# The columns of x and of the gate, taken out of a decode kernel's first load and fetched by 16 small DMAs on ScalarE's queue

## The chip, the cores and the metric

The kernel runs on one core of one Trainium2 chip. The metric is the device time of one execution in microseconds (us); of several runs the median is taken. A profile of one execution stands beside it: its instructions on TensorE (PE, with its weight loads PEld), VectorE (DVE), ScalarE (ACT), GpSimd (POOL) and SyncE (SP), and its DMAs.

## What is computed

One decode step of two attention blocks over the same token, mixed by a gate. Block A has 16 heads with a cache of their own each, block B 16 query heads over 8 cached heads; both have 8192 cached positions of 256 elements, and everything is float32.

```python
g = sigmoid((x * gate_w).sum(-1, keepdims=True))     # x: 1 x 448
# for A (16 cached heads) and B (8 cached heads, each for two query heads):
q = (x @ wq).reshape(heads, 256)
scores = einsum(q, k_cache) * 256 ** -0.5
o = einsum(softmax(scores), v_cache)
y = o.reshape(heads * 256) @ wo
out = g * y_A + (1 - g) * y_B
```

The caches and the weights are 432 MB; x and gate_w are 448 elements each.

## The kernel before

All inputs are laid out in one array in device memory, `stream`, in the order in which the kernel uses them. `plan()` (L47) makes that order: for each of 8 sets of heads a piece of `wq`, then 12 tiles of K (three units of four tiles each; 16 rows of 256 elements on 128 partitions a tile), the V tiles three places behind their K tiles, and the set's piece of `wo`. It cuts this list into loads of `FULL` = 15,872 columns of float32 on 128 partitions. `LOADS` has one entry for each buffer fill; the last fills consist of several smaller loads into regions of one buffer.

The buffers are the three slots of the pool `ring` (`SLOTS = 3`). The loop over `LOADS` at the end of the kernel takes a slot, issues the load's DMA on SP's queue (L468), and then calls `piece` for each piece in it, which writes out the instructions that consume it. The order is as written (`manual_schedule`): the framework adds semaphore waits but moves nothing. A load into a slot waits until the slot's previous contents have been read.

The small operands x and gate_w are called `xg`: each is held as 4 columns on 128 partitions (448 = 3 x 128 + 64, and the last 64 twice), so `XG` = 8 columns, 32 bytes a partition, 4 KB in all. Before, `plan` puts `("xg", 0)` first in the list, and its 8 columns are the first of the first load, which is therefore 15,880 columns wide; every slot has `FULL + XG` columns for that reason. When `piece` meets kind `"xg"`, it calls `inputs` on the first four columns and keeps the other four in `GW[0]`.

`inputs` (L191) copies x into the zeroed tile `xz` with three DVE copies (L192 to L194). `project` (L220) multiplies `xz` with `wq` on PE to give the queries of a set; ScalarE copies them out (L224) and `spread` prepares them. `prepare` computes the gate from `xz` and `GW[0]` (L200 to L205). The scores come from PE (`scores`, L255) or, for one unit of each set, from DVE (`scores_by_row`, L277 and L281), the sums over V from PE (`attend`, L307). Before all that, DVE and POOL make constants (L119 to L182), which needs no load. The output leaves with one DMA of four partitions (L483).

Of the kernel before, what the change touches and what calls it, by code (L numbers as in the profile page):

```python
# [7 lines left out]
F32 = mybir.dt.float32  # L8
# [6 lines left out]
P = 128  # L15
D = 448
DH = 256
SK = 8192
NCOL = SK // P
KF = D // P  # L20
# [5 lines left out]
ROWS = 16  # L26
NT = NCOL // ROWS
FULL = 15872
# [6 lines left out]
WQ = (4 * KF + 2) * DH  # L35
# [5 lines left out]


XG = 2 * (KF + 1)
ATOM = {"xg": XG, "k": 2 * DH, "v": 2 * DH, "wq": 2 * DH, "wo": D}


def plan():  # L47

    size = {"xg": XG, "k": ROWS * DH, "v": ROWS * DH, "wq": WQ, "wo": 8 * D}
    per = len(UNITS) * NT  # L50
    n = len(TILES)
    items = []
    for i in range(n + LEAD):
        if i == 0:
            items += [("xg", 0), ("wq", 0)]
        if i < n:
            items.append(("k", i))
        if i >= LEAD:
            items.append(("v", i - LEAD))
        if i % per == 7 and i // per + 1 < NS:  # L60
            items.append(("wq", i // per + 1))
        if i % per == LEAD + 1 and i >= per:
            items.append(("wo", i // per - 1))
    loads, room = [[]], FULL
    last = [("v", n - 3), ("v", n - 2)]
    for kind, i in items[:items.index(last[0])]:
        at, left = 0, size[kind]
        while left:
            step = min(left, room) // ATOM[kind] * ATOM[kind]
            if step:  # L70
                loads[-1].append((kind, i, at, step))
            at, left, room = at + step, left - step, room - step * (kind != "xg")
            if left:
                loads.append([])
                room = FULL

    loads = [[x] for x in loads]
    x = loads[-2][0]
    loads[-2] = [x[:2], x[2:]]
    loads[-1] += [[(kind, i, 0, size[kind])] for kind, i in last]  # L80
    at, end = 0, []
    for c in LAST_CUT:
        end.append([("v", n - 1, at, c * DH)])
        at += c * DH

    for h, e, n in ((3, 0, 2), (0, 0, 2), (1, 0, 3), (2, 1, 1)):
        end.append([("wo", NS - 1, (2 * h + e) * D, n * D)])
    return loads + [end]


LOADS = plan()


@with_exitstack
def kernel(
# [5 lines left out]
    nc = tc.nc  # L101
    scale = DH ** -0.5

    const = ctx.enter_context(tc.tile_pool(name="const", bufs=1))
    ring = ctx.enter_context(tc.tile_pool(name="ring", bufs=SLOTS))
# [85 lines left out]
    def inputs(xs):  # L191
        nc.vector.tensor_copy(xz[:, :KF, 0], xs[:, :KF])  # L192
        nc.vector.tensor_copy(xz[:KR, KF, 0:1], xs[:KR, KF:])  # L193
        nc.vector.tensor_copy(xz[KR:, KF + 1, 0:1], xs[KR:, KF:])  # L194

    def prepare(gw):
        clear(YY[0], D)
        gp = ps_s.tile([1, 1], F32, name="sm")
        for c in range(KF + 1):
            nc.tensor.matmul(gp, xz[:, c, 0:1], gw[:, c:c + 1], start=(c == 0), stop=(c == KF))  # L200
        ge = const.tile([1, 1], F32, name="ge")
        nc.scalar.activation(ge, gp, AF.Exp, scale=-1.0)
        nc.vector.tensor_scalar(ge, ge, 1.0, None, op0=OP.add)
        nc.vector.reciprocal(gate[:, 0:1], ge)
        nc.vector.tensor_scalar(gate[:, 1:2], gate[:, 0:1], -1.0, 1.0, op0=OP.mult, op1=OP.add)  # L205
# [5 lines left out]
    def project(s, c0, w):  # L211

        if c0 == 0:
            QR[s] = ps_s.tile([2 * BLK, 2 * DH], F32, name="sm")
        q = QR[s]
        for j in range(w.shape[1]):
            a, c = divmod(c0 + j, KF)
            for a in (a,) if a < 2 else (0, 1):
                c = c if c0 + j < 2 * KF else KF
                nc.tensor.matmul(q[BLK * a:BLK * (a + 1), :], xz[:, c if c < KF else KF + a, :], w[:, j, :],  # L220
                                 start=(c == 0), stop=(c == KF), skip_group_check=True)
        if c0 + w.shape[1] == 2 * KF + 1:
            QR[s] = small.tile([P, NB * BLK], F32, name="px")[:2 * BLK, :2 * DH]
            nc.scalar.activation(QR[s], q, AF.Copy)  # L224

    def spread(s):

        qt = ps_s.tile([P, 2, 2, 2], F32, name="sm")
        qr = QR.pop(s)
        for h in range(2):  # L230
            for e in range(2):
                at = h * DH + e * P
                nc.tensor.matmul(qt[:, h, e, :], qr[:, at:at + P], rows4[:2 * BLK, :2], start=True, stop=True)
        for r, a, h, M in ((2, 0, 0, 2), (0, 1, 0, 1), (1, 1, 1, 1)):
            if (s, r) in BY_ROW:
                qa = ps_s.tile([P, DH], F32, name="sm")
                nc.tensor.matmul(qa, spread32, qr[:, h * DH:(h + 1) * DH], start=True, stop=True)  # L237
                QA[s, r] = small.tile([P, DH], F32, name="qa", bufs=1)
                nc.scalar.activation(QA[s, r], qa, AF.Copy, scale=-scale)
                continue  # L240
            nc.vector.tensor_scalar(QB[s % 2, r][:, :, BLK:BLK + M], qt[:, h:h + M, :, a].rearrange("p h e -> p e h"),
                                    -scale, None, op0=OP.mult)
# [56 lines left out]
    def attend(u, t, j0, n, vt):  # L299

        w = 2 * NG * R[heads(u)]
        if t == 0 and j0 == 0:
            O[u] = ps_o.tile([P, 2 * DH], F32, name="o")
        pr = PR[u, t]
        for j in range(j0, j0 + n, 2):
            g = j // 2 % (P // w)
            nc.tensor.matmul(O[u][w * g:w * (g + 1), :], pr[:, j // 2, :w], vt[:, j - j0:j - j0 + 2, :],  # L307
                             start=(t == 0 and j < 2 * P // w), stop=(t == NT - 1 and j >= NB - 2 * P // w),
                             skip_group_check=True)
# [91 lines left out]
    LAST, GW = {}, {}  # L401
# [3 lines left out]
    def wait(n, f, *args):  # L405
        todo.append([n, f, args])

    def tick():
        for t in todo:
            t[0] -= 1  # L410
        for t in [t for t in todo if t[0] <= 0]:
            todo.remove(t)
            t[1](*t[2])

    def piece(kind, i, at, view):
        n = view.shape[-1] // ATOM[kind]
        j0 = at // ATOM[kind]
        if kind == "xg":
            inputs(view[:, :KF + 1])
            GW[0] = view[:, KF + 1:]  # L420
        elif kind == "wq":
            project(i, j0, view.rearrange("p (c n) -> p c n", c=n))
            if j0 + n < 2 * KF + 1:
                pass
            elif i == 0:
                spread(0)
                prepare(GW[0])
            else:
                wait(1, spread, i)
        elif kind == "k":  # L430
            u, t = TILES[i]
            if u in BY_ROW:
                scores_by_row(u, t, 2 * j0, view.rearrange("p (j d) -> p j d", d=DH))
            else:
                scores(u, t, j0, view.rearrange("p (c n) -> p c n", c=n))
            if j0 + n < 2 * NG:
                return
            tick()
            if t == NT - 1:
                gather(u)  # L440
                wait(1, combine, u)
                wait(2, column, u)
        elif kind == "v":
            u, t = TILES[i]
            n = view.shape[-1] // DH
            attend(u, t, at // DH, n, view.rearrange("p (j d) -> p j d", d=DH))
            if at // DH + n == ROWS:
                if t == NT - 1:
                    take(u)
                    if u != TILES[-1][0]:  # L450
                        wait(1, project_o, u)
                if i >= len(TILES) - LEAD:
                    tick()
        elif kind == "wo" and i < NS - 1:
            emit_set(i, j0, view.rearrange("p (c n) -> p c n", c=n))
            if i == NS - 2 and j0 + n == 8:
                fold()
        else:
            for j in range(n):
                LAST[divmod(j0 + j, 2)] = view[:, j * D:(j + 1) * D]  # L460

    off = 0
    for fill in LOADS:
        buf = ring.tile([P, FULL + XG], F32, name="slot")
        c = 0
        for load in fill:
            n = sum(x[3] for x in load)
            nc.sync.dma_start(buf[:, c:c + n], stream[off:off + P * n].rearrange("(p n) -> p n", p=P))  # L468
            off += P * n
            for x in load:  # L470
                piece(*x[:3], buf[:, c:c + x[3]])
                c += x[3]
# [78 lines left out]
```

## Time and profile before

| what | value |
|---|---|
| median of 3 runs | 1010.5 us (1010.24 to 1010.51) |
| span of the profiled execution | 1008.4 us |
| what the median has beyond that span | 2.1 us |
| DMA | 432.49 MB, mean 429 GB/s |
| PE busy | 584.2 us (58%) |
| DVE busy | 458.2 us (45%) |
| ACT busy | 92.8 us (9%) |
| DMA issues by SP | 63 loads at L468, 1 output at L483 |

The span runs from the first to the last instruction of the profiled execution; the time of a run is counted a little wider, and no separate time of the profiled execution is given, so the median stands for it. In the rows, an engine's name with a q (SPq) is its instruction queue, which waits, branches and issues DMAs. A row of the timeline has start, duration, engine, line, operation, output<-input and count; what stands in brackets is how long the engine was idle before it and what ended that. A row of the windows has, for a stretch, the busy time of PE, PEld, DVE, ACT and POOL, the granted clock of PE, the DMA engines' busy share and GB/s. A row of the waits has the total, how often, and the longest.

### The profile page before, as it was taken

What the parts mean: (1) busy time and instruction counts of PE and PEld (TensorE: products, weight loads), DVE (VectorE), ACT (ScalarE), POOL (GpSimd) and SP (SyncE); (2) the same over time, 40 slices, a digit from 0 to 9 for tenths busy, and PEclk for the clock granted to TensorE, in tenths of its full rate; (3) what the DMA queues carried; (4) which work ended last, traced back from release to release, by engine and by line L of the source; (5) the groups of instructions that cost most, each with busy time, mean ns of one, the idle gap of its engine ahead of it and who ended that gap; (6) DMA issues with size and microseconds to landing.
All of it is one profiled execution on the core that took longest, in us unless ns stands there. A gap on an engine that the chain in (4) does not pass through costs nothing.

```text
span 1008.4 us, 7568 instructions
## 1 busy us (share of the span) xinstructions
PE 584.2 (58%) x3154; PEld 171.4 (17%) x3154; DVE 458.2 (45%) x644; ACT 92.8 (9%) x307; POOL 1.9 (0%) x10
## 2 busy tenths in 40 slices
PE   0855845664655555746646576655665637536567
PEld 0211211121111111212111121111211112111112
DVE  1386213961248521576214841248521585206851
ACT  0100100010100110001100000100110100101010
POOL 0000000000000000000000000000000000000000
PEclk9877787777787787877777767776787867877878
DMA  9999999999999999999999999999999999999997
GB/s 403 442 438 418 434 436 439 418 441 431 441 436 426 424 441 438 429 426 442 431 428 441 431 429 434 436 434 431 432 431 441 439 423 424 439 443 431 418 426 310
DMA packets 9113, 432.49 MB, mean 429 GB/s; under 512 B 1016, under 2 KB 1144, under 8 KB 1784
## 3 DMA queue, kind: packets, MB, share of 16 engines
q1 hardware_dynamic: 9080, 432.02, 99.2%
q8 instruction: 24, 0.39, 0.2%
q14 instruction: 9, 0.07, 0.0%
HBM read 432.02 MB, written 0.00 MB: 428 GB/s over the span
## 4 chain that ended last, share of the span: by engine, by line
DMA 72%; DVE 15%; PE 11%; ACT 1%; issue 1%; another core or an unknown queue 0%; SPq 0%; ACTq 0%; DVEq 0%
DMA slot<-in_stream_dram 72%; DVE sr L281 6%; DVE slot L277 6%; PE o L307 5%; PE sc L255 4%; PE sm L220 1%; ACT px L264 0%; DVE mn L261 0%; DVE pr L294 0%; ACT pxr L290 0%; DVE pr L267 0%; ACT ew L346 0%; DVE wr L353 0%; PE sm L371 0%; DVE mt L287 0%
## 5 line engine op out<-in xcount | busy, mean ns | idle before, releaser
L307 PE MATMUL o<-slot,pr 128*32 128x512 f32 (+1 forms) x1536 | 352.4, 764 | 220.2 <-DMA slot<-in_stream_dram 220.2
L255 PE MATMUL sc<-slot,qb 128*32 128x512 f32 x1024 | 199.0, 725 | 102.5 <-DMA slot<-in_stream_dram 102.3
L261 DVE TENSOR_REDUCE mn<-sc 128x1 f32<-128x512 f32 x64 | 44.1, 690 | 334.3 <-PE sc L255 311.5
L277 DVE TENSOR_TENSOR slot<-slot,qa 128x4096 f32<-128x4096 f32 (+7 forms) x40 | 142.6, 3565 | 43.6 <-DMA slot<-in_stream_dram 43.6
L307 PEld LDWEIGHTS o<-slot,pr 128*32 128x32 f32 (+1 forms) x1536 | 80.6, 143 | 403.5 <-DMA slot<-in_stream_dram 249.0
L281 DVE TENSOR_REDUCE sr<-slot 128x16 f32<-128x4096 f32 (+7 forms) x40 | 142.7, 3567 | 1.4
L255 PEld LDWEIGHTS sc<-slot,qb 128*32 128x32 f32 x1024 | 47.1, 132 | 221.2 <-issue 125.5
L264 ACT ACTIVATE px<-sc,st 128x512 f32<-128x512 f32 x64 | 44.0, 687 | 408.1 <-DVE st L262 366.5
L267 DVE STREAM_TRANSPOSE pr<-px 128x512 f32<-128x512 f32 x64 | 45.6, 713 | 59.5 <-ACT px L264 59.5
L220 PE MATMUL sm<-slot,xz 128*32 128x512 f32 x128 | 47.2, 717 | 36.8 <-DVE xz L193 22.9
L290 ACT ACTIVATE pxr<-sr,st 128x16 f32<-128x16 f32 x32 | 9.8, 308 | 372.9 <-DVE st L288 372.9
L371 PE MATMUL sm<-sel,ob 128*128 128x1 f32 (+1 forms) x96 | 18.2, 294 | 36.6 <-DVE ob L317 36.6
L317 DVE SCALAR_TENSOR_TENSOR ob<-o,half,ob 128x256 f32<-128x256 f32 x24 | 11.3, 473 | 43.6 <-ACT ob L316 43.6
L371 PEld LDWEIGHTS sm<-sel,ob 128*128 128x128 f32 x96 | 16.2, 237 | 60.5 <-DVE ob L317 54.9
L220 PEld LDWEIGHTS sm<-slot,xz 128*32 128x32 f32 x128 | 11.3, 129 | 67.0 <-issue 28.4
L294 DVE TENSOR_TENSOR pr<-pxr,cols 128x256 f32<-128x256 f32 x32 | 13.6, 426 | 15.9 <-ACT pxr L290 15.9
L237 PE MATMUL sm<-px,spread 64*128 64x256 f32 x16 | 7.1, 533 | 14.4 <-DVE es L347 14.4
L360 PE MATMUL sm<-ones,wr 1*128 1x1 f32 x48 | 9.6, 268 | 9.2 <-DVE wr L353 9.2
L316 ACT ACTIVATE ob<-o,half 128x256 f32<-128x256 f32 x24 | 11.3, 469 | 39.7 <-PE o L307 39.6
L380 PE MATMUL Y<-slot,ocs 128*1 128x448 f32 x112 | 14.1, 621 | 0.0
L360 PEld LDWEIGHTS sm<-ones,wr 1*128 1x128 f32 x48 | 7.8, 203 | 32.6 <-issue 32.6
L264 ACT ACTIVATION_READ_ACCUMULATOR px<-sc,st 128x1 f32 x64 | 12.3, 193 | 0.0
(73 smaller groups left out, 137.5 us busy)
## 6 DMA issues: line engine op xcount, KB each, us to landing
slot<-in_stream_dram SPq DMA_DIRECT2D x50, 7936.0 KB, 42.5
slot<-in_stream_dram SPq DMA_DIRECT2D x1, 7940.0 KB, 21.8
slot<-in_stream_dram SPq DMA_DIRECT2D x1, 4864.0 KB, 41.2
slot<-in_stream_dram SPq DMA_DIRECT2D x2, 2048.0 KB, 25.3
slot<-in_stream_dram SPq DMA_DIRECT2D x1, 3072.0 KB, 30.1
slot<-in_stream_dram SPq DMA_DIRECT2D x1, 1280.0 KB, 20.8
slot<-in_stream_dram SPq DMA_DIRECT2D x1, 1024.0 KB, 23.5
slot<-in_stream_dram SPq DMA_DIRECT2D x2, 512.0 KB, 24.8
```

The costliest lines, as they stand in the source:

```text
L220: nc.tensor.matmul(q[BLK * a:BLK * (a + 1), :], xz[:, c if c < KF else KF + a, :], w[:, j, :], start=(c == 0), stop=(c == KF), skip_group_ ...
L255: nc.tensor.matmul(sc[32 * g:32 * (g + 1), :], qb[:, e, at:at + 32], kt[:, j, :], start=(e == 0), stop=(e == 1), skip_group_check=True)
L261: nc.vector.tensor_reduce(mn, sc, axis=AX.X, op=OP.min)
L264: nc.scalar.activation(px, sc, AF.Exp, bias=st[:, 0, t:t + 1], scale=-1.0, accum_out=st[:, 1, t:t + 1])
L267: nc.vector.transpose(pr.rearrange("p (q r k) -> p q k r", r=BLK, k=2), px.rearrange("p (q k c) -> p q k c", c=BLK, k=2))
L277: nc.vector.tensor_tensor(kt, kt, QA[u][:, None, :].to_broadcast([P, n, DH]), op=OP.mult)
L281: nc.vector.tensor_reduce(sc[:, j0:j0 + n], kt, axis=AX.X, op=OP.add)
L294: nc.vector.tensor_tensor(pr, px[:, :, None, :].to_broadcast([P, ROWS // 2, NG * NT, 2]), cols[:, t].rearrange("p g r -> p (g r)")[:, None ...
L307: nc.tensor.matmul(O[u][w * g:w * (g + 1), :], pr[:, j // 2, :w], vt[:, j - j0:j - j0 + 2, :], start=(t == 0 and j < 2 * P // w), stop=(t ...
L360: nc.tensor.matmul(cl, WR.pop(u).rearrange("p c x m k -> p (c x m k)"), ones[:1, :], start=True, stop=True)
L371: nc.tensor.matmul(oc[:, e, :M], OB[u][:, e::2], SEL[u][:, :M], start=True, stop=True)
L380: nc.tensor.matmul(YY[0][32 * h:32 * h + 1, :], OC[s, r][:, e, m:m + 1], wt[:, j, :], start=False, stop=(s == NS - 2 and e == 1), skip_gro ...
```

## The change

The kind `"xg"` leaves the plan. The 8 columns get a tile of their own, `xg` in the pool `const`. They stand at the head of `stream`, 128 rows of 32 bytes, and are fetched by 16 DMAs on ScalarE's queue, with 1, 2, 3, ... 15 and then 8 partitions (120 + 8 = 128). These stand in program order ahead of the loop over `LOADS`. `inputs` is called, and `GW[0]` set, right after the first load has been issued, on the new tile. The first load is 15,872 columns wide, as most others are, and the slots are `FULL` columns wide.

```diff
 XG = 2 * (KF + 1)
-ATOM = {"xg": XG, "k": 2 * DH, "v": 2 * DH, "wq": 2 * DH, "wo": D}
+SMALL = list(range(1, 16)) + [8]
+ATOM = {"k": 2 * DH, "v": 2 * DH, "wq": 2 * DH, "wo": D}
...
         if i == 0:
-            items += [("xg", 0), ("wq", 0)]
+            items.append(("wq", 0))
...
-            at, left, room = at + step, left - step, room - step * (kind != "xg")
+            at, left, room = at + step, left - step, room - step
...
-        if kind == "xg":
-            inputs(view[:, :KF + 1])
-            GW[0] = view[:, KF + 1:]
-        elif kind == "wq":
+        if kind == "wq":
...
-    off = 0
+    xg = const.tile([P, XG], F32, name="xg")
+    row = 0
+    for n in SMALL:
+        nc.scalar.dma_start(xg[row:row + n, :], stream[row * XG:(row + n) * XG].rearrange("(p n) -> p n", n=XG))
+        row += n
+
+    off = P * XG
     for fill in LOADS:
-        buf = ring.tile([P, FULL + XG], F32, name="slot")
+        buf = ring.tile([P, FULL], F32, name="slot")
         c = 0
         for load in fill:
             n = sum(x[3] for x in load)
             nc.sync.dma_start(buf[:, c:c + n], stream[off:off + P * n].rearrange("(p n) -> p n", p=P))
             off += P * n
+            if off == P * (XG + FULL):
+                inputs(xg[:, :KF + 1])
+                GW[0] = xg[:, KF + 1:]
             for x in load:
```

More of the change, by code (lines that the diff above doesn't have):

```diff
@@ L43 @@
 XG = 2 * (KF + 1)
-ATOM = {"xg": XG, "k": 2 * DH, "v": 2 * DH, "wq": 2 * DH, "wo": D}
+SMALL = list(range(1, 16)) + [8]
+ATOM = {"k": 2 * DH, "v": 2 * DH, "wq": 2 * DH, "wo": D}
 def plan():
-    size = {"xg": XG, "k": ROWS * DH, "v": ROWS * DH, "wq": WQ, "wo": 8 * D}
+    size = {"k": ROWS * DH, "v": ROWS * DH, "wq": WQ, "wo": 8 * D}
     per = len(UNITS) * NT
@@ L530 @@
     }
-    parts["xg"] = [_np.concatenate([col(get("A_x")), col(get("gate_w"))], axis=1)]
+    xg = _np.concatenate([col(get("A_x")), col(get("gate_w"))], axis=1)
     laid = {
-        "stream": _np.concatenate([
+        "stream": _np.concatenate([xg.ravel()] + [
             _np.concatenate([parts[kind][i][:, at:at + n] for kind, i, at, n in load], axis=1).ravel()
```

## The prediction

> **What bounds the kernel now.** I read the page first: the span, the slices of the DMA engines, the queues and the chain that ended last.
>
> ```profile
> span 1008.4 us, 7568 instructions
> DMA  9999999999999999999999999999999999999997
> q1 hardware_dynamic: 9080, 432.02, 99.2%
> DMA 72%; DVE 15%; PE 11%; ACT 1%; issue 1%; another core or an unknown queue 0%; SPq 0%; ACTq 0%; DVEq 0%
> ...
> slot<-in_stream_dram SPq DMA_DIRECT2D x50, 7936.0 KB, 42.5
> slot<-in_stream_dram SPq DMA_DIRECT2D x1, 7940.0 KB, 21.8
> slot<-in_stream_dram SPq DMA_DIRECT2D x1, 1280.0 KB, 20.8
> ```
>
> The queue's packets fill 99.2% of 16 engines' time. The chain names PE and DVE too, but only because a load is issued when they release a slot; such a load then waits some 42.5 us although a load alone lands in 21.8, so it stands behind another load. The windows confirm that this cover never runs out between start and tail:
>
> ```profile
> 0.00:30.00 30.00, 6.44 (x16) 1.35 (x16) 5.00 (x32) 1.87 (x2) 1.90 (x10) 1.00 0.96 406
> ...
> 60.00:100.00 40.00, 24.22 (x90) 7.15 (x90) 30.05 (x21) 2.21 (x9) 0.00 (x0) 0.71 1.00 432
> 100.00:500.00 400.00, 232.69 (x1270) 68.63 (x1266) 175.73 (x245) 37.45 (x124) 0.00 (x0) 0.76 1.00 433
> 500.00:960.00 460.00, 269.61 (x1407) 78.50 (x1405) 214.42 (x283) 41.30 (x139) 0.00 (x0) 0.75 1.00 432
> 960.00:1008.40 48.40, 31.53 (x263) 9.83 (x262) 15.27 (x33) 5.51 (x19) 0.00 (x0) 0.80 0.86 365
> ```
>
> The last two figures of each row are the DMA share and GB/s: 1.00 at 432 to 433 from 60 to 960 us. The time is therefore the first load's start, plus 432 MB at a fixed rate, plus a short tail. Whatever delays the first load's issue is paid in full, since no later gap could take it up; whatever touches PE, DVE or ACT costs nothing while slots come free early enough.
>
> **How an issue can be held.** Next I read SP's issues one by one, and who else woke at the same moments.
>
> ```profile
> 0.74 1.34 SPq L468 DMA_DIRECT2D slot<-in_stream_dram  x3
> 941.08 0.80 SPq L468 DMA_DIRECT2D slot<-in_stream_dram  x2
> 964.99 1.28 SPq L468 DMA_DIRECT2D slot<-in_stream_dram  x3
> 974.62 1.75 SPq L468 DMA_DIRECT2D slot<-in_stream_dram  x4
> 982.70 0.33 SPq L468 DMA_DIRECT2D slot<-in_stream_dram  x1
> 985.78 0.33 SPq L468 DMA_DIRECT2D slot<-in_stream_dram  x1
> 990.68 0.33 SPq L468 DMA_DIRECT2D slot<-in_stream_dram  x1
> ...
> 982.72 0.20 PEld L307 LDWEIGHTS o<-slot,pr 128*32 128x32 f32 x8 [6.50 <-DMA slot<-in_stream_dram]
> 990.70 0.16 PEld L307 LDWEIGHTS o<-slot,pr 128*32 128x32 f32 x8 [1.22 <-DMA slot<-in_stream_dram]
> ...
> 964.99 20.77 DMA slot<-in_stream_dram
> 985.78 18.75 DMA slot<-in_stream_dram
> ...
> SPq L468 <- DMA slot<-in_stream_dram: 13.6, 3, 6.3
> ```
>
> The last fill is one buffer cut into seven regions, issued as x4 at 974.62 and then singly at 982.70, 985.78 and 990.68. All seven have the same free buffer, so the last three wait for something else. The waits view of 960 to 992 us calls it a DMA, three times, 13.6 us together. Counted backwards, the single at 985.78 is the eighth after the first of the three issued at 964.99, and the chain has that one landing 20.77 us later, at 985.76. The single at 990.68 is the eighth after the second of those three, at the moment at which PE, too, is woken by a DMA (990.70). The single at 982.70 is the eighth after the second of the two from 941.08; PE is woken at 982.72. So in this program a DMA is issued only when the eighth DMA before it has landed: eight completion counters are handed out in turn, and one is not used again while its DMA is under way.
>
> **The change part by part.** *Removed:* eight of 15,880 columns of the first load (4 KB of 7,940 KB, 0.01 us of 21.8) and 32 B of each slot. Nothing.
>
> *Moved:* x's three copies (L192 to L194) now wait for the 16 small DMAs, not for the load.
>
> ```profile
> 0.73 1.28 ACT L224 ACT_TABLE_LOAD   x1 [0.73 <-PEq L537]
> 29.39 0.59 ACT L224 ACTIVATE px<-sm 64x512 f32<-64x512 f32 x1 [27.37 <-PE sm L220]
> 22.68 0.17 DVE L192 COPY xz<-slot 128x3 f32<-128x3 f32 x1 [16.65 <-DMA slot<-in_stream_dram]
> 22.90 1.06 PE L220 MATMUL sm<-slot,xz 128*32 128x512 f32 x1 [22.90 <-DVE xz L193]
> 41.43 1.08 PE L255 MATMUL sc<-slot,qb 128*32 128x512 f32 x4 [3.67 <-DMA slot<-in_stream_dram]
> 61.62 4.43 DVE L277 TENSOR_TENSOR slot<-slot,qa 128x4096 f32<-128x4096 f32 x1 [1.74 <-DMA slot<-in_stream_dram]
> 37.82 0.33 SPq L468 DMA_DIRECT2D slot<-in_stream_dram  x1
> 1005.89 0.65 SPq L483 DMA_DIRECT2D out_dram<-ys  x1
> SPq L546 <- DMA out_dram<-ys: 0.7, 1, 0.7
> ```
>
> DVE idles 16.65 us at that point and PE needs the load's columns anyway, so an early x gains at most the 0.2 us from 22.68 to PE's start at 22.90, behind a DMA stream that doesn't wait for PE here. Nothing.
>
> *Added on ACT:* 16 issues, then (or before them) the table load, then the activation at 29.39. ACT idles 27.37 us there; sixteen issues at 0.45 to 0.80 us are 7 to 13 us. Hidden. Queued behind a waiting issue on ACT are only the rest of the sixteen and that activation.
>
> *Added on SP, without an edit there:* in program order the 16 small DMAs stand ahead of the first load. Numbering them 0 to 15, the first load takes the same counter as number 8 and may be issued only when number 8 has landed. Behind it on SP stand loads two and three, and with them the whole stream; every engine's first real work waits for it. Number 8 itself waits for number 0, which has landed by then. The start of the first load, 0.74 us before, becomes ACT's start + 8 issues + the landing of one small DMA.
>
> - ACT's start: its first entry is at 0.73, SP's at 0.74; the same. If the sequencer runs the table load first and stands still for it, 1.28 later. Between 0 and 1.28 I take 0, since a table load belongs in front of the activation whose line it carries.
> - Pitch of issues: no ACT issue is in the trace. SP's bursts give 1.34 for three and 1.75 for four, 0.45 each; a single issue takes 0.33 with 128 partitions, 0.65 for the output with 4. The small DMAs, of 1 to 9 partitions, resemble the output most, so I take 0.60, with 0.33 and 0.80 (0.65 and the 0.1 by which burst issues exceed single ones, rounded up) as ends. [...] By the burst rows alone eight issues would be 3.6 us, by the output's row 5.2.
> - Landing: the output's wait bounds it from below: 0.65 for the issue and 0.7 of waiting give 1.35; from above, 1005.89 to the span's end at 1008.4, 2.5. A read may be slower: the first load landed in 21.8 us, of which one load's pitch, 22.68 to 41.43, is 18.75, and 3.1 are fixed. I take 2.0, with 1.35 and 3.1 as ends.
>
> Sum: 8 x 0.60 + 2.0 = 6.8 us. Low end 8 x 0.33 + 1.35 = 4.0; high end 8 x 0.80 + 3.1 + 1.28 = 10.8.
>
> *After that:* numbers 9 to 12 are under way by then, 13 to 15 may mix with the first load's rows (128 rows on 16 engines are eight each, 18.75 / 8 = 2.34 us a row) and land a few rows later, at about 20 us, before that load does at 29. Loads two to eight take the counters of numbers 9 to 15 and are due long after. 256 tiny packets and completions cost the engines a few tenths at most, mostly while they are idle. Every later issue keeps its place modulo eight (16 is twice eight), so the tail is unchanged. Slots come free the same time after their landings, so nothing absorbs the shift.
>
> The span of the profiled execution goes from 1008.4 to 1015.2; the median of the runs, 1010.5, lies 2.1 above that span, which I keep: 1017.3.
>
> **The rivals.** *The two queues are counted apart.* Then SP issues at 0.74 as before and the small DMAs run beside the first load. Against it: the waits seen attach to a DMA's completion and not to a buffer; for it: only SP issues in this trace, so a common count isn't shown. If each small packet takes a turn with a row of 2.34 us, an engine that serves all sixteen ends at about 3 + 16 x 2.34 = 40 us. The fourth load's issue stood at 37.82 with x at 22.68; to keep the engines fed it must come 3.1 before 61.6 (the third load's landing, which DVE awaits), so x may be 58.5 - 37.8 = 20.7 us late, until 43. At 40 nothing is lost: 1010.5 to 1011.5, no change. [...] Chance 0.08.
>
> *Counted apart, and x comes too late.* If data and completion each take a turn, x is there at 3 + 32 x 2.34 = 78 us; past the deciding point of 43 every microsecond is lost, 35 in all: 1045. Nothing in the trace has a second queue with many small packets. Chance 0.03.
>
> *The edit does little either way, and the start gains.* The first load without x might spread its first packets sooner; of the fixed 3.1 us at most 1 or 2 could go. Around 1009, faster. It needs counters apart and idle small DMAs. Chance 0.02.
>
> **How the numbers follow.** The forecast has 0.87; its ends give 1014.5 and 1021.3, and I let the range run from 1014.3 to 1021.5, which leaves out the rivals (0.13) and little else. A measurement of this kernel tells about 0.2% (2 us) from no change. Faster 0.02, same 0.08, slower 0.90.
>
> **What would show it.** Right: SP's first issue at 6 to 9 us instead of 0.74, waiting for a DMA into xg; ACT's first nine issues back to back from about 0.74; DVE's copies at L192 well before the first landing; the first landing at 28 to 31, the same later rows shifted by one amount, and DMA share 1.00 as before. Wrong: a first SP issue at 0.74 (then the queues are counted apart, and x's landing decides), a DMA share under 1.00 between 60 and 960, or a shift that grows or shrinks along the span.

## The result, and the profile after

The changed kernel takes 1016.63 us (median of 4 runs, 1015.71 to 1017.38) against 1010.37 before; the ratio is 1.0061, 95% interval 1.0047 to 1.0075. It is 6.3 us slower; 6.8 were forecast, and 1016.63 lies near the 1017.3 predicted. The path to that number, however, was another one than the prediction's. The profiled execution took 1017.38 us, 2.0 over its span; it was the longest of the four.

From the page after: the span, the load queue, and ScalarE's queue with its 256 packets (128 of 32 bytes, the rows of data, and 128 of 4 bytes, called completions here: before, SP's queue has 1012 such packets, and the trace 1013 updates of semaphores by DMAs).

```profile
span 1015.4 us, 7594 instructions
...
q1 hardware_dynamic: 9080, 432.02, 98.8%
...
q10 hardware_dynamic: 256, 0.00, 0.0%
```

The start of the kernel after, from timelines of ACT, SP and all engines (L463 issues the small DMAs, L472 the loads):

```profile
0.73 2.83 ACTq L463 DMA_DIRECT2D xg<-in_stream_dram  x8
0.74 0.40 SPq L472 DMA_DIRECT2D slot<-in_stream_dram  x1
22.56 3.16 ACTq L463 DMA_DIRECT2D xg<-in_stream_dram  x8
23.83 0.81 SPq L472 DMA_DIRECT2D slot<-in_stream_dram  x2
25.75 1.28 ACT L225 ACT_TABLE_LOAD   x1 [25.75 <-DMA xg<-in_stream_dram]
45.31 0.17 DVE L193 COPY xz<-xg 128x3 f32<-128x3 f32 x1 [39.29 <-DMA slot<-in_stream_dram]
61.11 0.33 SPq L472 DMA_DIRECT2D slot<-in_stream_dram  x1
```

The first load is issued at 0.74, as before: it is not held. ACT issues eight small DMAs and then stands still until 22.56, when the first load has landed (0.74 + 21.80 = 22.54 in the chain below). The second and third loads, issued within 1.34 us of the first before, come from 23.83 on. The waits and the chain say whom SP waited for, and that this is on the path that set the end:

```profile
SPq L472 <- DMA xg<-in_stream_dram: 22.7, 1, 22.7
...
0.74 21.80 DMA slot<-in_stream_dram
23.83 21.48 DMA slot<-in_stream_dram
45.54 7.11 PE sm L221 x16
```

Before, the chain had the second load under way from 1.20 to 41.30:

```profile
1.20 40.10 DMA slot<-in_stream_dram
```

In windows of the kernel before and then of the kernel after (the last two figures are the DMA share and GB/s):

```profile
20.00:30.00 10.00, 6.44 (x16) 1.35 (x16) 0.36 (x3) 0.59 (x1) 0.00 (x0) 1.00 0.94 406
60.00:75.00 15.00, 10.51 (x32) 3.16 (x32) 12.77 (x8) 0.40 (x2) 0.00 (x0) 0.73 0.96 415
75.00:940.00 865.00, 506.09 (x2695) 147.94 (x2695) 391.17 (x529) 79.41 (x265) 0.00 (x0) 0.75 1.00 433
...
100.00:125.00 25.00, 20.33 (x122) 6.92 (x122) 7.01 (x19) 3.52 (x10) 0.00 (x0) 0.76 1.02 443
```

```profile
20.00:30.00 10.00, 0.00 (x0) 0.00 (x0) 0.00 (x0) 1.28 (x1) 0.00 (x0) 1.00 0.56 203
60.00:75.00 15.00, 10.41 (x62) 2.75 (x54) 12.08 (x13) 2.33 (x6) 0.00 (x0) 0.99 0.98 404
75.00:940.00 865.00, 497.52 (x2694) 146.51 (x2698) 399.75 (x546) 79.89 (x270) 0.00 (x0) 0.76 1.00 433
...
100.00:125.00 25.00, 22.18 (x135) 8.01 (x139) 14.69 (x23) 3.28 (x12) 0.00 (x0) 0.82 1.01 435
```

Between 20 and 30 us the bytes of (406 - 203) x 10 / 433 = 4.7 us are missing; the second load lands at 45.31 instead of 41.30. Between 60 and 75, where the fourth load follows its late issue at 61.11, another (415 - 404) x 15 / 433 = 0.4 us are missing. Between 100 and 125, where a few rows of 2.4 to 3.1 us stand at about 101 us, it is (443 - 435) x 25 / 433 = 0.5. A further part lies in no gap. It is spread over the span: by the trace's packet records, a full row of 63,488 bytes takes 2344.3 ns on average before and 2347.2 after (rows between 75 and 940 us, the few over 2420 ns left out). An engine moves 432.02 MB / 16 / 63,488 B = 425 such rows, so 2.9 ns a row are 1.2 us. 4.7 + 0.4 + 0.5 + 1.2 = 6.8 us, of the 7.0 by which this execution's span is longer (1015.4 against 1008.4). The medians differ by 6.3.

### The profile page after: what moved, and what is told of

Read it like the earlier page. It is cut to its first block, busy times and chain, and to the rows that moved or that the text cites. A ratio compares the mean times of both kernels' runs of the same rounds, so it can differ in the third digit from the quotient of the medians.

```text
span 1015.4 us, 7594 instructions
## 1 busy us (share of the span) xinstructions
PE 567.5 (56%) x3154; PEld 167.9 (17%) x3154; DVE 457.7 (45%) x644; ACT 92.6 (9%) x307; POOL 1.9 (0%) x10
## 3 DMA queue, kind: packets, MB, share of 16 engines
q1 hardware_dynamic: 9080, 432.02, 98.8%
HBM read 432.02 MB, written 0.00 MB: 425 GB/s over the span
## 4 chain that ended last, share of the span: by engine, by line
DMA 69%; DVE 16%; PE 13%; ACT 2%; issue 1%; ACTq 0%; SPq 0%; DVEq 0%
DMA slot<-in_stream_dram 69%; DVE slot L278 6%; DVE sr L282 6%; PE o L308 6%; PE sc L256 5%; PE sm L221 1%; ACT px L265 1%; DVE mn L262 1%; DVE pr L268 1%; DVE pr L295 0%; ACT pxr L291 0%; PE sm L238 0%; ACT ew L347 0%; DVE mt L288 0%; PE sm L361 0%
## 5 line engine op out<-in xcount | busy, mean ns | idle before, releaser
L308 PE MATMUL o<-slot,pr 128*32 128x512 f32 (+1 forms) x1536 | 340.6, 745 | 207.1 <-DMA slot<-in_stream_dram 207.1
L256 PE MATMUL sc<-slot,qb 128*32 128x512 f32 x1024 | 193.4, 714 | 97.3 <-DMA slot<-in_stream_dram 96.6
```

Source lines behind the costliest of these rows:

```text
L256: nc.tensor.matmul(sc[32 * g:32 * (g + 1), :], qb[:, e, at:at + 32], kt[:, j, :], start=(e == 0), stop=(e == 1), skip_group_check=True)
```

## The experiments

The theory from these rows: counters are shared by SP's and ACT's queues, but handed out in another order than the prediction took: first small DMA, first load, the other 15 small DMAs, then the second load. So the small DMA number 9 has the first load's counter and waits until that has landed; loads two and three have the counters of numbers 9 and 10 and wait for these. The kept trace bears this out: it names the semaphore, that is the counter, of each DMA. The first small DMA has 100, the first load 102, the next six small ones 103 to 108, number 8 again 100, number 9 again 102, and the second load 102 after it; from number 8 on, every small DMA and the second and third load first wait for the semaphore that they take. Why the framework hands them out in this order isn't shown. The rivals: the late x (45.3 us instead of 22.7) costs the time; or the many small packets cost it as such. A third term, the slots' addresses in the on-chip memory, was taken up when the rows turned out slower: the new tile of 32 bytes moves the slots, which started 0, 64 and 32 bytes off multiples of 256 before, to 32 bytes off such a multiple, all three.

### Seven and eight small DMAs

```diff
-SMALL = list(range(1, 16)) + [8]
+SMALL = [16] * 6 + [32]
```

> Seven small DMAs on ACT instead of 16 (six of 16 partitions, one of 32). Theory (shared counters): in the order in which counters are handed out the first load is number 1, behind the first small DMA, so loads two and three are numbers 8 and 9; number 8 waits only for the first small DMA (landed at about 2 us). The second load is issued in the first microseconds and the DMA engines have no gap at 22 us. x lands at about 34 us (13 turns of 2.34 us beside load rows), which the slots' slack still covers. Before + 1.4 us from the slots' addresses (all three now at an odd multiple of 32 bytes): 1011.8 us. Rival (a late x is what costs): x is 11 us later than before, half of the lateness in the changed kernel, so about half of its 6.3 us: 1013.5 us.

```diff
-SMALL = list(range(1, 16)) + [8]
+SMALL = [16] * 8
```

> Eight small DMAs of 16 partitions on ACT, one more than in the run with seven. Theory (shared counters): the second load becomes number 9 and shares its counter with the first load, so it is issued only when that one has landed, at 22.6 us; the DMA engines stand still for about 2 us and restart slowly, 3.2 us in all, 1.2 less than in the changed kernel, whose second load comes at 23.83. With 1.4 us for the slots' addresses: 1015.0 us, 3.2 above the run with seven. Rival (a late x is what costs): x lands no later than 23 us, as the engines are free from 22.2 on, so this run is no slower than the one with seven: 1010.4 to 1011.8 us.

Measured: with seven 1011.34 us (ratio to before 1.0009, 1.0000 to 1.0018), with eight 1014.42 (1.0041, 1.0029 to 1.0054). One DMA more costs 3.1 us. Timelines of the run with seven, then of the one with eight, with a window of the latter:

```profile
0.74 7.90 SPq L472 DMA_DIRECT2D slot<-in_stream_dram  x2
22.53 0.33 SPq L472 DMA_DIRECT2D slot<-in_stream_dram  x1
36.57 0.17 DVE L193 COPY xz<-xg 128x3 f32<-128x3 f32 x1 [30.55 <-DMA xg<-in_stream_dram]
```

```profile
0.74 0.39 SPq L472 DMA_DIRECT2D slot<-in_stream_dram  x1
22.36 0.81 SPq L472 DMA_DIRECT2D slot<-in_stream_dram  x2
20.00:30.00 10.00, 6.70 (x16) 1.44 (x16) 0.36 (x3) 0.00 (x0) 0.00 (x0) 1.00 0.80 305
23.07 0.17 DVE L193 COPY xz<-xg 128x3 f32<-128x3 f32 x1 [17.05 <-DMA xg<-in_stream_dram]
```

With seven, two loads are issued within 8 us and the third, number 9, waits for the first load's landing, which hurts nobody: another load is under way. With eight, it is the second load that is number 9, and the engines run dry (305 GB/s between 20 and 30 us, against 406 with seven). x comes at 36.6 in the faster run and at 23.1 in the slower one, so a late x as such is not what costs; the second load's place in the count is. Nor do the many small packets cost it: ScalarE's queue carries 240 of them with seven DMAs and 256 with eight. In the run with seven the second load was issued at 8.3, not in the first microseconds: SP waited 7.2 us for a DMA into `xg`, its counter's, which landed later than I expected, beside the first load's rows.

### The small DMAs on SP, ahead of the first load

```diff
-        nc.scalar.dma_start(xg[row:row + n, :], ...
+        nc.sync.dma_start(xg[row:row + n, :], ...
```

> The 16 small DMAs on SP's queue, ahead of the first load. Now the first load itself is held, as the prediction had assumed for ACT: its issue comes after 16 issues of 0.40 us each, at about 7.2 us, 6.5 later than before; x lands before it and no other gap follows. Theory (a later first load is paid in full): 1010.4 + 6.5 + 1.4 (addresses) = 1018.3 us. Rival (the slack of later loads takes up part of a late start): less than 1015 us.

Measured: 1017.33 us (1.0065, 1.0053 to 1.0078).

```profile
0.74 5.65 SPq L463 DMA_DIRECT2D xg<-in_stream_dram  x16
6.43 1.30 SPq L472 DMA_DIRECT2D slot<-in_stream_dram  x3
```

The first load is issued 5.7 us later than before (6.43 against 0.74), and the kernel takes 6.9 us more; its rows take 2347.5 ns, 3.2 more than before, which is 425 x 3.2 = 1.4. 5.7 + 1.4 is 7.1: the late start is paid in full. This is the late start that the prediction had described, but it comes from sixteen issues of 0.36 us in line on one queue, and not from a wait for a counter.

### x later still, without a held load

```diff
-SMALL = list(range(1, 16)) + [8]
+SMALL = [96, 15, 17]
```

> Three small DMAs on ACT of 96, 15 and 17 partitions. Few enough that no load waits for a counter, so there is no gap at 22 us; but 17 partitions don't divide over the engines and their rows may all queue on one engine, each taking a turn with a load row of 2.34 us. Theory: x lands at about 50 us (20 turns), 5 us later than in the changed kernel; the fourth load is then issued at about 66 us, needed at 58, and 7.7 us are lost: 1010.4 + 1.4 (addresses) + 7.7 = 1019.5 us, as one gap at about 60 us. If the 17 rows go in one turn, x is there at 13 us and nothing is lost: 1011.8 us. Rival (small packets cost as such, wherever they fall): as many packets as the changed kernel, 1016.

```diff
-        nc.scalar.dma_start(xg[row:row + n, :], ...
+        nc.gpsimd.dma_start(xg[row:row + n, :], ...
```

> The 16 small DMAs on GpSimd's queue instead of ScalarE's. Theory: GpSimd's DMAs have counters of their own, so loads one to three are issued at 0.7 to 2 us as before and the gap at 22 us is gone. Each small DMA takes one or two turns beside load rows: with one, x is there at 41 us and nothing is lost: 1011.8 us; with two, at 78 us, and 35 us are lost: 1047 us. In either case SP's second issue is before 2 us. Rival (counters are shared by all queues): the second issue at about 24 us and 1016.6 us.

Measured: 1029.6 us (1.0188, 1.0175 to 1.0202) and 1031.51 us (1.0209, 1.0195 to 1.0223); both forecasts missed the size, because x came at another time. First the run with 96, 15 and 17 partitions, then the 16 DMAs on GpSimd's queue:

```profile
59.55 0.17 DVE L193 COPY xz<-xg 128x3 f32<-128x3 f32 x1 [53.52 <-DMA xg<-in_stream_dram]
74.29 0.33 SPq L472 DMA_DIRECT2D slot<-in_stream_dram  x1
60.00:80.00 20.00, 18.65 (x115) 5.42 (x113) 6.35 (x17) 4.24 (x11) 0.00 (x0) 1.00 0.27 102
```

```profile
0.74 1.33 SPq L472 DMA_DIRECT2D slot<-in_stream_dram  x3
3.35 4.24 POOL L463 DMA_DIRECT2D xg<-in_stream_dram  x8
12.72 0.52 POOL L463 DMA_DIRECT2D xg<-in_stream_dram  x1 [5.13 <-DMA xg<-in_stream_dram]
60.67 0.17 DVE L193 COPY xz<-xg 128x3 f32<-128x3 f32 x1 [54.61 <-DMA xg<-in_stream_dram]
76.17 0.33 SPq L472 DMA_DIRECT2D slot<-in_stream_dram  x1
60.00:80.00 20.00, 17.76 (x107) 5.30 (x109) 5.80 (x18) 3.47 (x9) 0.00 (x0) 1.00 0.16 51
```

The lost time agrees with the prediction's deciding point: the fourth load must be issued 3.1 us before the third has landed. By the packet records the third load lands at 59.6 us in the first of these runs and at 59.4 in the second, so the fourth, issued at 74.29 and 76.17, is 17.8 and 19.9 us late. Measured are 19.2 and 21.1; less some 1.4 for the slots' addresses, 17.8 and 19.7. Two things follow. A late x costs nothing as long as the fourth load's issue is in time (x at 36.6 us in the run with seven), and then every microsecond. In the changed kernel the third load itself lands only at 63.9, so the fourth, issued at 61.11, is 0.3 late: x at 45.3 costs about the 0.4 seen there. And GpSimd's DMAs have counters of their own: three loads are issued from 0.74 on without a wait, as the prediction's first rival had assumed for ACT, while GpSimd issues eight small DMAs and holds the ninth until one into `xg` has landed. The trace has semaphores 102 to 109 for these, and others for the loads.

Why x is late shows in the packet records. In the changed kernel small packets start at 7.28, 9.62, 11.97, 14.31, 16.66 and 19.00 us beside the first load's rows: data, completion, data, completion, one load row of 2.34 us apart. In the run with 17 partitions the last ones follow at the same pace up to 58.8. I read the pace as turns: one row of 62 KB of the load, one small packet, with a completion needing a turn of its own. The records name no engine, so that one engine takes them in turn is an inference from the pace.

### The slots' addresses

The changed kernel with `xg` padded, by 32 bytes (slots 64 bytes off a multiple of 256) and then by 224 (slots at multiples of 256):

```diff
-    xg = const.tile([P, XG], F32, name="xg")
+    xg = const.tile([P, 2 * XG], F32, name="xg")[:, :XG]
...
+    xg = const.tile([P, 8 * XG], F32, name="xg")[:, :XG]
```

> The changed kernel with its tile xg padded from 32 to 64 bytes a partition, which moves all three slots from an odd multiple of 32 bytes to a multiple of 64. Theory: a row of a load takes 2351 ns on average in the changed kernel and 2347 before, where two of three slots start at multiples of 64; with all three aligned a full load takes 18.72 us instead of 18.756, over 55 loads 2.0 us: 1014.6 us. The gap of the second load at 22 to 25 us stays. Rival (addresses don't matter; the gap alone makes up the 6.3 us): 1016.6 us.

> The changed kernel with its tile xg padded to 256 bytes a partition, so that all slots start at multiples of 256 bytes; the 16 small DMAs and the gap at 22 us stay. Theory (address): rows go from 2347.2 ns to about 2342.5, 8 x 4.7 ns on 55 loads, 2.1 us less: 1014.5 us. Rival (the rows are slower for another reason that comes with the separate xg, or the gap makes up all of the loss): 1016.3 to 1016.6 us.

The kernel before, with wider slots (0, 128 and 64 bytes off; then all at multiples of 256) and with a constant tile 32 bytes longer (32, 96 and 64 off):

```diff
-        buf = ring.tile([P, FULL + XG], F32, name="slot")
+        buf = ring.tile([P, FULL + 2 * XG], F32, name="slot")
...
+        buf = ring.tile([P, FULL + 8 * XG], F32, name="slot")
...
-    gate = const.tile([1, 2], F32, name="gate")
+    gate = const.tile([1, 2 + XG], F32, name="gate")
```

> The kernel before with its slots 32 bytes wider, so that all three start at multiples of 64 bytes (before, the middle one starts at an odd multiple of 32). Theory of the addresses: its third of the loads, 18, get 0.037 us faster each, 0.7 us: 1009.7 us. Rival (addresses don't matter): 1010.4 us.

> The kernel before with its slots 224 bytes wider, so that all three start at multiples of 256 bytes. Before, a row of 63,488 bytes takes 2342 to 2343 ns on average in two of the slots and 2346.5 in the middle one. Theory (the start address of a slot sets the time of its rows): all rows near 2342.5, a third of 55 loads 8 x 4 ns faster: 0.6 us less, 1009.8 us. Rival (the address doesn't matter): 1010.4 us and one slot still slower than the others.

> The kernel before with a constant tile 32 bytes longer, so that its slots start 32, 64 and 96 bytes off multiples of 256; nothing else differs. Theory (address): all three slots get rows of about 2346 to 2347 ns, 8 x 4 ns more on two thirds of 55 loads: 1.2 us more, 1011.6 us, without any small DMA. Rival (a second queue or the separate xg makes the rows slow): 1010.4 us.

One small DMA of 128 partitions, with `xg` padded in the same two ways:

```diff
-SMALL = list(range(1, 16)) + [8]
+SMALL = [128]
```

> x and gate as one DMA of 128 partitions on ACT, and xg padded to 64 bytes, so that all slots start at multiples of 64. Theory: one counter more in use, the second and third loads are issued at once, x lands within a few us, no gap; all loads at 18.72 us: 0.7 us under before, 1009.7 us. Rival (any second queue beside the loads costs): 1010.4 us or more.

> x and gate as one DMA of 128 partitions on ACT, slots at multiples of 256 bytes. Theory (address): against 1011.43 us with slots 64 bytes off such a multiple, rows of 2342.5 instead of 2346.6 ns take off 1.8 us: 1009.6 us, under the kernel before. Rival (address doesn't matter): 1011.4 us.

| kernel | slots' offsets from a multiple of 256 | mean row, ns | time, us | ratio to before (95%) |
|---|---|---|---|---|
| before | 0, 64, 32 | 2344.3 | 1010.4 | |
| before, pitch + 32 bytes | 0, 128, 64 | 2343.8 | 1010.07 | 0.9996 (0.9987 to 1.0005) |
| before, all at 256 | 0, 0, 0 | 2342.2 | 1008.92 | 0.9985 (0.9976 to 0.9994) |
| before, shifted by 32 | 32, 96, 64 | 2346.6 | 1011.14 | 1.0008 (0.9999 to 1.0017) |
| changed | 32, 32, 32 | 2347.2 | 1016.63 | 1.0061 (1.0047 to 1.0075) |
| changed, padded to 64 | 64, 64, 64 | 2346.2 | 1016.27 | 1.0057 (1.0045 to 1.0070) |
| changed, padded to 256 | 0, 0, 0 | 2342.0 | 1013.83 | 1.0035 (1.0023 to 1.0048) |
| one DMA, padded to 64 | 64, 64, 64 | 2346.6 | 1011.43 | 1.0009 (1.0000 to 1.0018) |
| one DMA, padded to 256 | 0, 0, 0 | 2342.1 | 1008.60 | 0.9983 (0.9974 to 0.9992) |

The row means are worked out from the packet records as above. In the profile, the same shows as one GB/s in the windows; the changed kernel padded to 256, then one DMA padded to 256:

```profile
75.00:940.00 865.00, 498.62 (x2721) 147.04 (x2723) 402.44 (x546) 80.67 (x271) 0.00 (x0) 0.77 1.00 434
```

```profile
75.00:940.00 865.00, 491.79 (x2695) 143.66 (x2695) 392.00 (x532) 79.58 (x265) 0.00 (x0) 0.77 1.00 434
```

My first form of the theory (multiples of 64 are enough) fell: padded to 64, the changed kernel gained 0.4 us where 2.0 were expected, and the single DMA was 1.0 us slower than before where it should have been 0.7 faster. The second form held: with all slots at multiples of 256 the rows take 2342 ns on average and the kernels gain 1.5 to 2.8 us (425 rows account for 0.9 of the 1.5 in the kernel before, for 2.2 of the 2.8 in the changed one and for 1.9 of the 2.8 with one DMA; the rest stays open). That the addresses slow the rows, and not the second queue, is shown by the kernel before shifted by 32 bytes: its rows take 2346.6 ns, nearly as long as the changed kernel's, with no small DMA in it (its time, 0.7 us more, can't be told from no change).

By what mechanism the addresses slow the rows is not shown. Only the destination is off: counted from the head of `stream`, the rows of all loads after the first start at multiples of 256 in all these kernels. The price of each offset stays open too: with all slots 32 bytes off a row took 5.2 ns more than with all at 256 (2347.2 against 2342.0, both with the changed kernel's small DMAs), with all 64 bytes off 4.2 more (2346.2); but in the kernel before, the slot 64 bytes off had rows of 2343 ns, while in the two kernels with all slots 64 bytes off, one slot starts at that very address, and its rows take 2346 to 2347.

The last row of the table is the fastest version found: one DMA for x and gate, slots at multiples of 256. It beats the changed kernel by 8.0 us and the one before by 1.9 (1010.46 in the same runs). That gain comes from the slots and not from taking x out of the first load: the kernel before with its slots at multiples of 256 takes 1008.92, within the scatter of it.

## Why the prediction was right, and where it was not

The direction and the size came out as forecast, but not by the forecast's path, and its own signs said so: it had named a first SP issue at 0.74 as a sign of being wrong, and there the issue stands. The sign's reading was wrong as well, since the queues are counted together all the same.

- *DMA sets the time, and a late stream is paid in full.* Right: with the start put off by 5.7 us on SP, nothing was taken up later.
- *A DMA is issued only when the eighth before it has landed, and ACT's and SP's queues count together.* Right, by the step from seven to eight small DMAs and by the semaphores in the trace. That GpSimd counts apart was not foreseen.
- *"In program order the 16 small DMAs stand ahead of the first load", so that the first load is held.* This step failed. The first load got the second number, not the seventeenth, and started at 0.74. Held was the second load, by a small DMA that was itself held by the first load's landing. The order in which code is written is not the order in which counters are handed out; the trace of before, with a single issuing queue, couldn't show that.
- *The price.* 8 x 0.60 + 2.0 = 6.8 us were forecast. Eight issues on ACT, of 1 to 8 partitions, took 2.83 us, 0.35 each, so the output's 0.65 was the wrong row to take the price from. A small DMA on idle engines landed within 1.27 us (22.56 to 23.83). By the prediction's own mechanism that would have been 4.1. What was paid instead, in the profiled execution, is 4.7 of missing bytes at 20 to 30 us, 0.4 at the fourth load, 0.5 at about 101 us and 1.2 in slower rows. That some load is held behind the shared count was foreseen. The near match of 6.8 and 6.3 is luck, and so is the range: none of the terms that it was added up from was paid, and most of the time went at another load's gap.
- *"32 B of each slot. Nothing."* Wrong by 1.2 us: the slots' addresses moved, and with them the time of every row.
- *x is there at about 20 us.* It came at 45.3, since eight of the small DMAs were held until 22.56 and four of those then took turns with the second load's rows. The prediction's rivals had the mechanism: turns for data and completion beside the load's rows, and a deciding point for the fourth load's issue. Their figures for x were 40 and 78 us with the queues counted apart; on GpSimd's queue, where they are, it was 60.7.

## What to carry to other kernels

Count the DMAs that are issued before the first big loads: in this program small transfers share eight completion counters with big ones (semaphores 100 and 102 to 108 in the changed kernel), and the ninth of the count waits for the first, across SP's and ACT's queues (there small DMA number 9, the tenth of the count, waited for the first load, the second of it, from 3.6 to 22.56 us). The order of the count isn't that of the code. One transfer of 128 partitions costs the count one place, 16 pieces cost the stream a gap. When a small tile is added beside large buffers, look where the buffers now start: keeping them at multiples of 256 bytes was worth 1.5 to 2.8 us of 1010 here, against 4.7 for the gap.

## What was not expected of the hardware

- With all destination buffers at multiples of 256 bytes a load's rows took 2342 ns; with all of them 32 or 64 bytes off, 2346 to 2347, 0.2% more.
- Beside the first load, small packets and their completions follow each other one load row of 2.34 us apart: six starts in a row from 7.28 to 19.00 us.
- After the gap the first rows of a load are slow: 2.4 to 3.7 us instead of 2.34 for the first row of the second load, as at the start of the kernel.
